# A token mixer behind gated linear attention on one core: u of batch 1 turned by DMA transposes, decays of batch 1 from products, and a new instruction list

## The chip, the cores and the metric

The kernel runs on one core of a Trainium2 chip. The metric is the device time of one execution in microseconds; smaller is better. The core has TensorE (PE, with its weight loads shown as PEld), VectorE (DVE), ScalarE (ACT), GpSimd (POOL) and SyncE (SP), each with its own instruction queue that runs in order, and 16 DMA engines that they share.

## The reference

Two stages follow each other. The first is a recurrent attention with a gate for each key channel; the second is an MLP-mixer block over its output.

```python
B, H, S, D = 4, 8, 768, 48
f = 1 / (1 + exp(-f_logit))
for t in range(S):
    state = f[:, :, t, :, None] * state + einsum('bhd,bhe->bhde', k[:, :, t], v[:, :, t])
    y[:, :, t] = einsum('bhd,bhde->bhe', q[:, :, t], state)
x = y.transpose(0, 2, 1, 3).reshape(B, S, H * D)              # (4, 768, 384)
h = maximum(x.transpose(0, 2, 1) @ w_tok1, 0) @ w_tok2        # 768 -> 256 -> 768
u = x + h.transpose(0, 2, 1)
out = u + maximum(u @ w_ch1, 0) @ w_ch2                       # 384 -> 1536 -> 384
```

Inputs and output are float32. Matmuls run in bf16 with float32 sums.

## The kernel before

**Attention.** The 768 steps are cut into six chunks of 128. Within a chunk the recurrence is closed: running sums of the log gates (a product with a triangle of ones, "sums") give G = exp(-sum) and Gi = exp(sum), q*G and k*Gi are formed ("gated"), both are turned by TensorE ("turn", then "turned" copies them from PSUM), their product ("scores") is masked by the triangle ("masked", AmT), and y is masked scores times v plus the turned q times the state before the chunk ("y", written as two bf16 blocks that "spread" makes, state_bd). The state goes on as `tsum = state + parts`, `state = tsum * glast`, where glast is the decay over the whole chunk. The log gate is kept as a bf16 high part and a low part ("lo", Llo, line 374), so "sums" has two matmuls of 384 columns (lines 456 and 457).

**Two ways to get the decay of a chunk.** If (batch, chunk) is in `TOTALS`, "sums" also has eight one-column matmuls against a column of ones (lines 450 to 455), and a small ScalarE exp of the result is glast (line 480). If not, ScalarE takes the exp of the last 32 rows of the sums ("grow", line 472) and a DMA from SP brings its last row into the form of glast (line 476). Before, only batch 0 is in `TOTALS`; it runs in pairs of chunks (`PAIRS`, function `pair`), with two-column matmuls of the same kind (line 607).

**Mixer.** For each batch: tok1 (line 750, 12 matmuls of 384 columns), h1T = relu (a copy from PSUM; batch 0 in two halves of 192 columns), tok2 (line 766), u = x + tok2 (line 782), u_bf in bf16, u turned to uT, ch1 (line 819, 24 groups of three matmuls), zT = relu (lines 352 and 354), ch2 (line 838, in pieces of four matmuls), the last sum (line 844) and a store from SP. For batches in `UTURN` u is turned by two DMA transposes from SP (line 795), each for three row blocks: the first for 0 to 2, the second for 3 to 5. For the others TensorE turns it by 18 transposes (line 804), which VectorE or ScalarE copy to uT.

**What sets the order.** Every step is recorded as an Op with the engines that can do it. The string `ORDER` lists them all once, by number, in one sequence. A letter behind a number picks the engine (A for ScalarE, D for VectorE, G for GpSimd), numbers behind colons the PSUM banks. `Plan.run` (line 123) issues the steps in that sequence, so each engine runs its own steps in the listed order; semaphores keep the dependences. So the list of one batch's mixer is interleaved with the attention of the next. The token `zN` stands for N filler matmuls of 512 columns (line 870) whose result nobody reads: 13 at the start and 17 more in the first 26 us.

**Loads.** q, k, v, f of batches 1 to 3 and the weights come by DMAs that GpSimd issues in list order; f of batch 0 comes from SP. Before anything else, constants are made (triangle, identity, masks, zeroed paddings), most of them by VectorE (lines 277 to 324).

Of the kernel before, what the change touches and what calls it, by code (L numbers as in the profile page):

```python
# [9 lines left out]
FP32 = mybir.dt.float32  # L10
# [5 lines left out]
NBANK = 8  # L16
RING = 16384
KEPT = 3
UTURN = (2, 3)
# [3 lines left out]
TOTALS = [(0, 0), (0, 1), (0, 2), (0, 3), (0, 4), (0, 5)]  # L23
# [4 lines left out]
POOLED = ()  # L28
LOADS0F = [('f', (0, 2)), ('f', (2, 4)), ('f', (4, 6))]
# [10 lines left out]
216:6 157 209 67 158 136A z3 193:2:5 164A 217 66 198 192:4:1 170 z1 161:0:2 63 196 195 197 z6 166 194:4 171A 172G 341  # L40
173 200 199:5:1 167A 201 174D 202A 203G 204 210 347 218 71 205D 206 338 211 219 207D 342 212 220 339 213 343G 221 214D
215A 222A 223D 232:3 344 168D 228:4 340G 233 348 229 240 234 224:0 345 241 68 230 244 225 243A 236 252:6 226 242A
250:7 349G 237 245 253D 251A 360:5 231 239A 248:6 346G 256:7 362 249D 368:4 238D 257A 272:6 65 246A 235 280:2 273A 227
254:3 363 396:7 281D 404:0 255A 364 247D 258:6 370 259A 262:2 74 361 270:1 263D 350 69 266:6 369 16 284:2 73 399 264:5
285D 400 260:3 72 271D 265A 302:2 267A 373 300:1 353 70 365 371 374:6 301D 354 48 366:5 372 375D 303A 306:1 261A 75
286:2 398 307D 296:3 367D 287A 355G 378:1 397 377:2 407 381 376:7 76 389 408 304:4 380 276:1 78 305A 388 274:7 405 387
383G 282:4 382A 351 79 278:2 379 283A 294:6 406 401 77 288:5 352D 295A 290:0 275A 409 402:6 277A 289D 291A 384:7 403D
292:1 386A 410:0 279A 390 293D 393:5 297A 392G 298:2 80 395A 411D 433:3 299A 394D 412:1 391G 436 413:4 385D 81 414:5
435 437 416 268:2 434 471:7 417 464:3 269A 424 441:1 472 328:2 425 313:0 415 418 323:4 426 420G 438 421:6 419G 324 82
427 423A 442 430:5 422A 84 325 432D 431A 465 443 439:6 83 326 473 444 314 440A 88 449:4 428A 445:1 452 86 429A 315  # L50
446D 466 453 447:4 448:5 454A 455G 451 467 85 329 450 474 318:4 87 459 456:6 460 319 457A 458D 461:5 316 468 475 462D
308:6 589 356 469 476 320 590 470D 586 477D 330 463D 587 493:7 598 321 481:5 588G 592 331 478:3 595 484:4 479 89 490:0
596 309 482 591D 483A 333:1 485 599 310 494 480A 486G 491 334 495G 597D 604:5 97 600D 487:3 605 496:0 500:7 606 94
498:4 497D 612:2 501D 492A 335 499D 614 488 593 510:4 609 615 530:3 594G 336 613 506:7 311 522:0 511A 93 601 617 610:2
523A 508:4 90 607 640:6 509D 608 518:0 641 91 611D 616 618:4 507A 516:1 531D 489A 92 519A 619D 648:5 504:3 517A 502:7
98 505D 643 620:0 503D 621:1 823 644 622:3 632 96 642 524:7 649 623 534:1 95 650 624 526:6 544:2 357 535D 527A 514:0
631 824 528:6 525A 515D 820 628:4 645 536:7 529A 630D 677:1 545A 646:6 625 537A 546:2 633 651 627G 647D 678 358 532:7
652 629A 653 540:0 626A 533D 547A 656:3 634 541A 658:4 680 654:2 661 659 602 636G 512:0 681 635A 99 520:7 679 662
637:5 513A 660 603G 554:1 655A 670 550:0 682 664G 556:6 639A 663G 521A 657:4 638A 693:3 668 555A 665:7 685:5 832 669
715:2 557 686 551D 687 683:4 667D 666A 708:5 688 829 538:0 671 821 558 539D 673A 822G 833 674:7 696 559 826 689:0 359  # L60
684A 716 548:3 690D 542:6 675D 676A 838:1 825D 543A 709 692:7 672A 549D 691:6 830 704 710 827 571:3 695 561:7 694 711
717 703 845:6 566:4 847 697 839 699G 700:0 846 831G 718 567 701D 841 848 562 698G 842 840 849 572 835 843 332 702D
705:1 327 552:6 706A 707D 317 712 719 828D 553A 844 576:0 720 713 573 721A 714D 872:2 574 722:5 875 737:6 850 731:3
876 738 734:1 851 563 723 739A 735 724A 577 732 736A 581:1 564 733G 834D 728:3 741 582 729 725:7 730A 568 726 874 583
727A 569 836 740 854:3 584 853:4:7 852:5:6 864 879:1 578 855 880 881 784:4 863 873 780:6 579 882 766:2 857 877 772:0
858G 865 907:1 878 773A 770:7 785A 774:0 767A 771D 760:4 859A 312 781D 910 786:7 322 761D 869:6 866 787A 762:4 856
868A 867G 775A 756:2 884 860:5 757A 744:0 885 908 778:7 745D 862A 886:2:3 837D 861A 911 888:0 763A 776:5 883 891 909
890 782:4 777A 892 750:1 779A 900 894G 768:5 783D 751A 893G 752:0 871A 889 914:4 753A 912 742:1 916 870D 895:0 769A
748:3 915 913 746:5 749A 887:4:6 897A 747D 921:7 337 758:2 898 575 788:5 899 759A 936:6 896A 810:3 789D 743A 917 943:0
904:5 919:1:4 918 905D 944 811 922 945 901 937 570 812 924 903A 902G 923 580 938 946 925 764:7 927G 754:1 765A 800:4  # L70
906A 755D 926A 920:5:7 939 932 795:1 931 928:2 801 929D 933:7 947 940 934A 935D 802 948 941 796 949A 942A 790:0 930A
959:6 965:5 950:2 966 962:7 797 967A 963 815:5 960 964G 951 961A 791 952A 969 816 956:6 953:7 957 805:2 565 798 958G
792 954 813 806 955G 803 817 968 793 807 1000:3 1004:7 1016:1 1005A 994:6 1001A 1017D 1002:7 818 1010:1 1003A 819
1014:5 1011D 794 986:7 1015D 799 976:1 987A 585 974:5 996:7 975D 982:3 808 980:5 995D 983A 809 1008:2 981D 560 998:6
977D 984:3 997D 999A 988:1 985A 972:6 989D 978:3 1009D 973A 970:1 1012:2 971A 990:6 1013D 1048:1 1006:7 991A 979A
1033:5 1007A 1038:3 1043:6 1034 1039 1023:7 1018:0 992:2 1049 1044 993A 1050 1040 1051 1052 1028:2 1041 1045 1042 1024
804 1035 814 1025 1036 1029 1046 1026 1047 1019 1027 1030 1037 1020 1031 1032 1021 1022
# [15 lines left out]
class Plan:  # L93
# [52 lines left out]
def kernel(  # L146
# [125 lines left out]

    def once(name, engine, fn, make, own, need=()):
# [16 lines left out]
    once("ident0", DVE, lambda: nc.vector.tensor_copy(ident[:, 0:1], tri_bf[:, 0:1]), ["ident"], 70, ["tri_bf"])  # L290
# [19 lines left out]
    if PAIRS:  # L310
# [3 lines left out]
        for n, rows in ((0, lo64), (1, hi64)):  # L314
            memset(f"half2{n}", half2[rows, n:n + 1], 1.0, ["half2"], 60)
            once(f"inc2{n}", DVE, lambda rows=rows: nc.vector.tensor_copy(inc2[rows, rows], tri_bf[rows, rows]), ["inc2"], 130,
                 ["tri_bf"])
            once(f"pmask0{n}", DVE, lambda rows=rows: nc.vector.tensor_copy(
                pmask[0][rows], tri_bf[rows, rows].unsqueeze(2).broadcast_to((64, 64, 2))), [("pmask", 0)], 200, ["tri_bf"])
        once("exc2", DVE, lambda: nc.vector.tensor_tensor(exc2, inc2, ident, ALU.subtract), ["exc2"], 150, ["inc2", "ident"])  # L320
        once("pmask1", DVE, lambda: nc.vector.tensor_copy(pmask[1], pmask[0]), [("pmask", 1)], 160, [("pmask", 0)])
        for n, rows in ((0, lo64), (1, hi64)):
            once(f"pmask1{n}", DVE, lambda rows=rows: nc.vector.tensor_copy(pmask[1][rows, :, 0], exc2[rows, rows]),
                 [("pmask", 1)], 130, ["exc2"])
# [16 lines left out]

    def copy_on(eng, out_, in_):
        if eng == ACT:
            nc.scalar.activation(out_, in_, AF.Copy, bias=0.0, scale=1.0)  # L344
        elif eng == DVE:
# [558 lines left out]
```

## Time and profile before

| what | us |
| --- | --- |
| median of 3 runs | 173.82 |
| lowest and highest | 173.77, 174.5 |
| span of the profiled execution | 172.8 |
| TensorE busy in the span | 164.4 |
| VectorE, ScalarE, GpSimd busy | 129.1, 109.7, 78.0 |

The profiled execution is shown by its span, from its first instruction to its last, 172.8 us; the median of the timed runs is 1.0 us above it, for what lies around the span. Sums in the prediction are made against the span and then moved by that 1.0. Columns of a group row: busy us in all, mean ns of one instruction, then the idle time of the engine just before them and what ended it. A row of a table of stretches gives for each stretch its length and, for each engine, busy us and number of instructions, then the granted clock, the DMA share and GB/s. Matmul durations include the drain of the pipeline, so the cost of a matmul in a row of them is read from start to start.

### The profile page before, as it was taken

The page shows a single profiled execution, that of the slowest core. Times are in us where ns is not written, and L with a number is a line of the kernel's source. Part 1 is how long each engine was busy: PE and PEld are TensorE (multiplying, and loading weights), DVE is VectorE, ACT ScalarE, POOL GpSimd, SP SyncE. Part 2 cuts the span into 40 slices and gives each one's busy share as a digit, 9 for nine tenths or more (in the row PEclk, how much of TensorE's full clock was granted, in tenths as well). Part 3 has the DMA queues.
Part 4 walks back from the last instruction along what each step waited for, and adds up shares of the span by engine and source line. Part 5 has one row for each costly group of instructions (what it writes and reads, how often), then busy time and mean ns, then how long its engine had stood idle before and what let it go on. Part 6 is the DMA issues. An engine that isn't in the chain of part 4 may idle for free.

```text
span 172.8 us, 4455 instructions
## 1 busy us (share of the span) xinstructions
PE 164.4 (95%) x1758; PEld 103.6 (60%) x1762; DVE 129.1 (75%) x287; ACT 109.7 (64%) x246; POOL 78.0 (45%) x102
## 2 busy tenths in 40 slices
PE   6889998999999999999999999999999999999991
PEld 2465755566676666676667566666565656656660
DVE  6989996978997789989969859887786355581132
ACT  3997938999893656799999685479933430444100
POOL 2999846998566893799663330010101012000000
PEclk9999999999999999999999999999999999999999
DMA  5999999999997998999999995638155006250054
GB/s 146 217 169 175 246 210 210 157 122 129 197 134 154 182 109 197 133 60 114 108 135 69 63 141 135 144 81 157 32 154 154 1 19 163 89 188 0 2 200 168
DMA packets 89573, 22.74 MB, mean 132 GB/s; under 512 B 82288, under 2 KB 88736, under 8 KB 89552
## 3 DMA queue, kind: packets, MB, share of 16 engines
q0 software_dynamic: 69600, 13.77, 91.7%
q1 hardware_dynamic: 19952, 8.69, 19.6%
q8 instruction: 14, 0.23, 0.6%
q14 instruction: 7, 0.06, 0.1%
HBM read 25.17 MB, written 4.72 MB: 173 GB/s over the span
## 4 chain that ended last, share of the span: by engine, by line
PE 75%; ACT 8%; DVE 5%; issue 1%; DVEq 0%
PE ps L838 26%; PE ps L819 23%; PE ps L750 4%; PE ps L766 4%; PE ps L408 3%; ACT zT L352 2%; PE ps L495 2%; PE ps L456 2%; PE ps L560 2%; PE ps L457 1%; ACT L L367 1%; PE ps L870 1%; PE ps L424 1%; PE ps L804 1%; PE ps L556 1%
## 5 line engine op out<-in xcount | busy, mean ns | idle before, releaser
L838 PE MATMUL ps<-w_ch,zT 128*128 128x384 bf16 (+2 forms) x300 | 52.9, 319 | 0.0
L819 PE MATMUL ps<-uT,w_ch 128*128 128x384 bf16 x288 | 52.4, 326 | 0.3 <-ACT GG L468 0.2
L352 ACT ACTIVATE zT<-ps 128x384 bf16<-128x384 f32 x61 | 28.2, 493 | 19.6 <-PE ps L819 14.6
L838 PEld LDWEIGHTS <-zT 128*128 128x128 bf16 x300 | 28.4, 98 | 17.4 <-issue 0.2
L819 PEld LDWEIGHTS <-w_ch 128*128 128x128 bf16 x288 | 26.9, 97 | 17.0 <-issue 0.7
L354 DVE TENSOR_SCALAR zT<-ps 128x384 bf16<-128x384 f32 x35 | 18.9, 554 | 10.4 <-PE ps L819 8.9
L536 DVE TENSOR_TENSOR AmT<-ps,tri_bf 128x512 bf16<-128x512 f32 x36 | 23.1, 683 | 2.3 <-PE ps L408 2.1
L348 POOL CAST state_bd<-state 48x192 bf16<-48x192 f32 x24 | 9.0, 376 | 34.6 <-DVE state L549 22.2
L844 DVE TENSOR_TENSOR x_nat<-x_nat,ps 128x384 f32<-128x384 f32 (+2 forms) x25 | 12.8, 534 | 10.3 <-PE ps L838 9.8
L264 POOL DMA_DIRECT2D qk_sb<-in_q_dram x16 | 15.9, 1000 | 0.8 <-issue 0.8
L264 POOL DMA_DIRECT2D qk_sb<-in_k_dram x16 | 15.7, 983 | 0.3 <-issue 0.3
L264 POOL DMA_DIRECT2D v_sb<-in_v_dram x16 | 15.7, 983 | 0.1
L782 DVE TENSOR_TENSOR x_nat<-x_nat,ps 128x384 f32<-128x384 f32 x21 | 10.8, 549 | 4.2 <-PE ps L766 4.1
L750 PE MATMUL ps<-x_bf,w_tok 128*128 128x384 bf16 x48 | 13.2, 326 | 0.3 <-DVE zT L698 0.2
L348 POOL CAST u_bf<-x_nat 128x384 bf16<-128x384 f32 x6 | 3.0, 506 | 20.7 <-DVE x_nat L782 20.7
L374 POOL TENSOR_TENSOR Llo<-L 128x384 bf16<-128x384 f32 x10 | 8.2, 826 | 6.4 <-ACT L L367 6.3
L485 DVE TENSOR_TENSOR qk<-qk_sb,GG 128x768 bf16<-128x768 bf16 x18 | 9.9, 555 | 1.4 <-ACT GG L468 1.4
L870 PE MATMUL ps<-x_nat 128*128 128x512 bf16 x26 | 8.7, 460 | 2.0 <-DVE x_nat L279 1.5
L466 ACT ACTIVATE GG<-ps 128x384 bf16<-128x384 f32 x18 | 8.7, 492 | 2.5 <-PE ps L457 2.3
L344 ACT ACTIVATE x_bf<-ps 128x384 bf16<-128x384 f32 x13 | 6.5, 499 | 5.9 <-PE ps L560 5.0
L766 PE MATMUL ps<-h1T,w_tok 128*128 128x384 bf16 x48 | 9.4, 326 | 0.8 <-ACT h1T L352 0.6
L468 ACT ACTIVATE GG<-ps 128x384 bf16<-128x384 f32 x18 | 8.9, 492 | 1.8 <-PE ps L457 1.6
(96 smaller groups left out, 266.4 us busy)
## 6 DMA issues: line engine op xcount, KB each, us to landing
out_dram<-x_nat SPq DMA_DIRECT2D x23, 192.0 KB, 2.2
f_sb<-in_f_logit_dram POOLq DMA_DIRECT2D x3, 1152.0 KB, 11.1
f_sb<-in_f_logit_dram SPq DMA_DIRECT2D x3, 384.0 KB, 4.2
w_ch<-in_moe_w_ch_dram POOLq DMA_DIRECT2D x2, 576.0 KB, 13.2
qk_sb<-in_q_dram POOLq DMA_DIRECT2D x12, 96.0 KB, 6.6
qk_sb<-in_k_dram POOLq DMA_DIRECT2D x12, 96.0 KB, 5.6
v_sb<-in_v_dram POOLq DMA_DIRECT2D x12, 96.0 KB, 4.5
w_ch<-in_moe_w_ch_dram POOLq DMA_DIRECT2D x1, 1152.0 KB, 10.0
```

What stands on the lines that cost most here:

```text
L264: lambda eng=eng, into=into, of=of: eng.dma_start(out=into, in_=of),
L348: nc.gpsimd.tensor_copy(out_, in_)
L352: nc.scalar.activation(out_, in_, AF.Relu, bias=0.0, scale=1.0)
L354: nc.vector.tensor_scalar(out_, in_, 0.0, None, ALU.max)
L536: add(("masked", b, c, p), DVE, lambda half=half, made=made: nc.vector.tensor_tensor(half, made(), tb4, ALU.mult), need=["tri_bf"], make=[ ...
L750: add(("tok1", b, rt, kt), PE, lambda rt=rt, kt=kt, pm=pm: nc.tensor.matmul(banks[pm.at][:, 0:DM], lhsT=w_tok1[:, kt, rt * 128:(rt + 1) * ...
L766: nc.tensor.matmul(banks[pm.at][:, 0:DM], lhsT=w_tok2[:, kt, tt * 128:(tt + 1) * 128], rhs=h1T[:, kt, :], start=(kt == 0 and not held), st ...
L782: nc.vector.tensor_tensor(to, un, banks[pm.at][:, 0:DM], ALU.add)
L819: nc.tensor.matmul(banks[pm.at][:, 0:384].rearrange("p (n t) -> p n t", t=128), lhsT=w[:, kt, c0:c0 + 128], rhs=uT[:, rows3, kt, :], start ...
L838: nc.tensor.matmul(banks[pm.at][:, 0:n1 - n0], lhsT=zT[:, kt, tt * 128:(tt + 1) * 128], rhs=w_ch2[:, kt, n0:n1], start=(kt == 0), stop=(kt ...
L844: add(("sum", b, tt, n0), DVE, lambda un=un, pm=pm, n=n1 - n0: nc.vector.tensor_tensor(un, un, banks[pm.at][:, 0:n], ALU.add), make=[("x_n ...
L870: nc.tensor.matmul(banks[NBANK - 1][0:rows, 0:cols], lhsT=steady[:, 0:rows], rhs=steady[:, 0:cols], start=True, stop=True)
```

## The change

- `UTURN` takes in batch 1: its u is turned by two DMA transposes from SP, and its 18 transposes and six copies to uT go.
- `TOTALS` takes in chunks 0 to 4 of batch 1: five times eight one-column matmuls and a small exp come, five grow steps and their five DMAs go. The paddings that these matmuls read are zeroed by new memsets.
- h1T of batch 0 is copied in whole rows (two copies of 384 columns in place of four of 192).
- The step state = tsum * decay may be listed for GpSimd; the list does so for chunks 2, 3 and 4 of batch 0 and chunk 1 of batch 2.
- Memsets may be listed for GpSimd, and copies among the constants for ScalarE.
- A token `wN` is one float32 filler matmul of N columns; it takes the place of the bf16 fillers at the start. The new list starts with `w512 w512 w384 s16` (`s16`: sixteen of 64 columns) and has no other filler.
- `ORDER` is another list throughout.

```diff
-UTURN = (2, 3)
+UTURN = (1, 2, 3)
-TOTALS = [(0, 0), (0, 1), (0, 2), (0, 3), (0, 4), (0, 5)]
+TOTALS = [(0, 0), (0, 1), (0, 2), (0, 3), (0, 4), (1, 0), (1, 1), (1, 2), (1, 3), (1, 4), (0, 5)]
+HALVES = False
+STATES = (DVE, POOL,)
...
     def memset(name, tl, value, make, own):
-        once(name, DVE, lambda: nc.vector.memset(tl, value), make, own)
+        op = once(name, (DVE, POOL), None, make, own)
+        op.fn = lambda: (nc.gpsimd if op.engine == POOL else nc.vector).memset(tl, value)
+
+    def copied(name, out_, in_, make, own, need):
+        op = once(name, (DVE, ACT), None, make, own, need)
+        op.fn = lambda: copy_on(op.engine, out_, in_)
...
+    def decayed(b, c, gb, key):
+        op = add(("state", b, c), STATES, None, need=["tsum", key], make=["state"], kind=("el", HP * D, True, 1))
+        op.fn = lambda: (nc.gpsimd if op.engine == POOL else nc.vector).tensor_tensor(state, tsum, gb, ALU.mult)
...
-            half = DM // 2 if b == 0 else DM
+            half = DM // 2 if b == 0 and HALVES else DM
...
     def idle(n, cols):
+        if not cols:
+            wide = spare[:, 0:512].bitcast(FP32)
+            nc.tensor.matmul(banks[NBANK - 1].rearrange("p (a n) -> p a n", n=128)[:, 0:n // 128], lhsT=wide[:, 0:128],
+                             rhs=wide[:, 0:128].unsqueeze(1).broadcast_to((128, n // 128, 128)), start=True, stop=True)
+            return
```

The two lists by stretch, each from the first tok2 of a batch to that of the next, as numbers of steps on an engine (before, then after):

| list up to | TensorE | VectorE | ScalarE |
| --- | --- | --- | --- |
| tok2 of batch 0 | 47, 50 | 74, 75 | 43, 55 |
| tok2 of batch 1 | 94, 86 | 63, 57 | 63, 58 |
| tok2 of batch 2 | 94, 91 | 69, 71 | 76, 75 |
| tok2 of batch 3 | 76, 78 | 50, 53 | 47, 35 |
| the end | 60, 60 | 30, 32 | 16, 12 |

Ahead of tok2 of batch 0 TensorE's new list has sums of chunks 0, 1 and 2 of batch 1 more. GpSimd's loads, in the order of the two lists:

```
before: q k v | k q q v v k of batch 0, w_tok1, f.1, w_tok2, w_ch1 (2), q.1.0 q.1.1 k.1.1 k.1.0 ...
after:  q k v | q k v k q of batch 0, f.1, k.1.0, v.0.4, w_tok1, w_tok2, q.1.0 k.1.1 q.1.1, w_ch1 (2), ...
```

SP's list around the new transposes: `glast.2.0 ut.1.0 glast.2.1 ut.1.1 glast.2.2 glast.2.3 store.0.0`.

More of the change, by code (lines that the diff above doesn't have):

```diff
@@ L40 @@
[L40 to L44, printed above, removed]
@@ L78 @@
+1015
 """
@@ L271, in load_w, with copy_on @@
             make=[name], kind=("load", 900, 1024, size))
+    def copy_on(eng, out_, in_):
+        if eng == ACT:
+            nc.scalar.activation(out_, in_, AF.Copy, bias=0.0, scale=1.0)
+        elif eng == DVE:
+            nc.vector.tensor_copy(out_, in_)
+        else:
+            nc.gpsimd.tensor_copy(out_, in_)
     def once(name, engine, fn, make, own, need=()):
@@ L548, in rest @@
                     need=["state"], make=["tsum"], bank=p_d, kind=small)
-                add(("state", b, c), DVE, lambda: nc.vector.tensor_tensor(state, tsum, gb, ALU.mult),
-                    need=["tsum", ("glast", g4)], make=["state"], kind=small)
+                decayed(b, c, gb, ("glast", g4))
             spread(b, c)
@@ L729, in pair @@
                         need=["state"], make=["tsum"], bank=p_d[k], kind=small)
-                    add(("state", 0, c), DVE, lambda gb=gb: nc.vector.tensor_tensor(state, tsum, gb, ALU.mult),
-                        need=["tsum", ("gpair", i2)], make=["state"], kind=small)
+                    decayed(0, c, gb, ("gpair", i2))
                 spread(0, c)
```

105 lines of the change are left out of this document (50 added, 55 removed).

## The prediction

> **What bounds the kernel now.** I read the busy totals first, then the chain that ended last, then a table cut where each batch's second token product (tok2, L766) begins: 30.0, 66.1, 104.9 and 137.8 us; the last matmul ends by 169.2.
>
> ```profile
> PE 164.4 (95%) x1758; PEld 103.6 (60%) x1762; DVE 129.1 (75%) x287; ACT 109.7 (64%) x246; POOL 78.0 (45%) x102
> PE 75%; ACT 8%; DVE 5%; issue 1%; DVEq 0%
> core 0: us, PE busy (x) PEld busy (x) DVE busy (x) ACT busy (x) POOL busy (x), PEclk, DMA share, GB/s
> 0.00:30.00 30.00, 25.80 (x451) 15.73 (x456) 25.02 (x74) 21.67 (x44) 21.92 (x33) 1.00 1.36 196
> 30.00:66.10 36.10, 35.77 (x382) 23.21 (x382) 31.36 (x64) 28.55 (x67) 29.43 (x36) 1.00 1.76 146
> 66.10:104.90 38.80, 38.52 (x402) 25.26 (x400) 32.84 (x70) 31.75 (x73) 22.35 (x26) 1.00 1.61 119
> 104.90:137.80 32.90, 32.90 (x325) 20.21 (x323) 25.11 (x51) 20.18 (x47) 2.76 (x7) 1.00 0.48 103
> 137.80:169.20 31.40, 31.39 (x205) 19.20 (x203) 14.26 (x29) 7.57 (x16) 1.53 (x3) 1.00 0.31 100
> ```
>
> From 30 us on TensorE is busy 99%: there time is TensorE work, and only less work saves any. Before 30 us it is busy 25.80 of 30.00, part of that with the fillers of L870; VectorE (25.02) and ScalarE (21.67) set that start. So I take two sums: T, when tok2 of batch 0 starts, and TensorE's work behind T.
>
> **Work behind T.** The costs, start to start:
>
> ```profile
> 71.16 0.50 PE ps L804 x9
> 145.76 10.72 PE ps L819 x66
> 9.52 0.17 PE L607 MATMUL ps<-x_nat,L 128*128 128x2 bf16 x1
> 9.89 0.16 PE L607 MATMUL ps<-x_nat,Llo 128*128 128x2 bf16 x1
> ```
>
> A transpose costs 0.50/9 = 0.056 us, a 384-column matmul 10.72/66 = 0.162, so a ch2 piece of four 0.65 and the two matmuls of a sums step 0.33. A two-column matmul costs (9.89-9.52)/15 = 0.025. Eighteen transposes of batch 1 go: -1.0. Five totals of eight one-column matmuls come: 40 x 0.025 = +1.0. The named edits cancel on TensorE; the list decides. Counting each list between its tok2 starts:
> - batch 0 to 1: three sums steps fewer (now ahead of T), -1.0; two totals, +0.4; five ch2 pieces fewer, -3.25: 36.1 becomes 32.25.
> - batch 1 to 2: two ch2 pieces more, +1.3; one sums step more, +0.33; transposes -1.0: 38.8 becomes 39.4.
> - batch 2 to 3: three ch2 pieces more, +1.95; one sums step fewer, -0.33: 32.9 becomes 34.5.
> - batch 3 to the end: the same 60 steps, 31.4.
>
> The sum falls from 139.2 to 137.6: **-1.6 us**. It comes from three sums steps with totals being done ahead of T, in holes.
>
> Is it still TensorE that sets these stretches? Prices of what changes engine:
>
> ```profile
> L354 DVE TENSOR_SCALAR zT<-ps 128x384 bf16<-128x384 f32 x35 | 18.9, 554 | 10.4 <-PE ps L819 8.9 <-ACT x_nat L344 1.5
> L346 DVE COPY qkT<-ps 128x1024 bf16<-128x1024 bf16 x9 | 6.2, 686 | 0.4 <-PE ps L495 0.4
> L485 DVE TENSOR_TENSOR qk<-qk_sb,GG 128x768 bf16<-128x768 bf16 x18 | 9.9, 555 | 1.4 <-ACT GG L468 1.4
> L346 DVE COPY uT<-ps 128x384 bf16<-128x384 bf16 x7 | 2.2, 352 | 0.3 <-PE ps L804 0.2
> L374 DVE TENSOR_TENSOR Llo<-L 128x384 bf16<-128x384 f32 x8 | 4.4, 561 | 0.0
> L374 POOL TENSOR_TENSOR Llo<-L 128x384 bf16<-128x384 f32 x10 | 8.2, 826 | 6.4 <-ACT L L367 6.3
> L468 ACT ACTIVATE GG<-ps 128x384 bf16<-128x384 f32 x18 | 8.9, 492 | 1.8 <-PE ps L457 1.6
> L472 ACT ACTIVATE grow<-ps 32x384 f32<-32x384 f32 x15 | 7.1, 482 | 1.0 <-PE ps L457 0.7
> L625 ACT ACTIVATE gpair<-ps 128x8 f32<-128x8 f32 x3 | 0.6, 205 | 0.0
> ```
>
> Other 384-column copies and sums on VectorE I take at 0.55 too. From batch 0 to 1 it has eight steps fewer (three x_nat, two of the 1024-column turns, one each of u, product, sum, h1T and memset go; a zT, an x_bf and two uT come), 3.8 us: 27.5 of 32.25 us, 85% (87% now). From batch 1 to 2 four zT, a sum, a turn, an x_bf, a product and a memset come, five uT, a Llo and a state product go, +2.3: 35.1 of 39.4, 89% (85% now). ScalarE sheds five grow steps (-2.4) for five small ones (+1.0) and nine zT. So TensorE still binds, with VectorE close behind in the second stretch.
>
> **The u transfers of batch 1.**
>
> ```profile
> L795 SPq DMA_TRANSPOSE uT<-u_bf x4: 1283/1289/1294, 108.6 to 144.3; - x4
> DMA to landing us min/median/max: 2.8/2.8/2.9
> ```
>
> In the new list SP has glast.2.0, ut.1.0, glast.2.1, ut.1.1. From tok2 of batch 1 at 0, at half a microsecond a step: ScalarE's ln.2.0 ends at 0.9, VectorE's lo.2.0 and three u at 2.9, GpSimd's two u_bf at 3.9, ScalarE's four gate steps, grow.2.0 and u_bf.1.0 at 3.4; SP issues at about 4, and it lands 2.8 later, at 6.8. Before the first ch1 of batch 1 the list gives TensorE twelve tok2 matmuls (1.9), ten ch2 pieces (6.5), five sums steps (1.7), three turns of eight (1.3) and scores, parts and a y (some 1.5): 13 us. The second transfer waits for u_bf.1.3 on ScalarE (8.4) and for u_bf.1.5 behind a 2.2 us issue on GpSimd; it lands near 11.3, its first reader is near 18. So it is hidden; without that cover the first would cost up to 6.8. Behind ut.1.1 on SP stand glast.2.2 and stores, not due soon.
>
> **T.** What binds the start:
>
> ```profile
> 4.26 0.84 ACT L387 ACTIVATE f_sb<-f_sb 128x768 f32<-128x768 f32 x1 [2.24 <-DMA f_sb<-in_f_logit_dram]
> 26.13 0.36 ACT L344 ACTIVATE state_bd<-state 48x192 bf16<-48x192 f32 x1 [3.07 <-PE ps L736]
> 9.88 1.17 DVE L629 TENSOR_TENSOR qk<-qk_sb,GG 128x384 bf16<-128x384 bf16 x4 [0.64 <-DMA qk_sb<-in_k_dram]
> 9.88:30.00 20.12, 17.79 (x42) 1.00 1.46 205
> L730 DVE TENSOR_TENSOR state<-tsum,gpair 128x192 f32<-128x192 f32 x4 | 1.4, 354 | 0.2
> L367 ACT ACTIVATE L<-f_sb 128x384 f32<-128x384 f32 x18 | 9.0, 517 | 0.2
> ```
>
> ScalarE's list ahead of T grows from 43 steps to 55: four more G and Gi (2.0), four constants (taken at 0.25, between the 0.205 and 0.492 of the rows above; 1.0), three exp and ln (1.55), a glast, a spread, the full-row h1T less an x_bf (0.45), 5.0 in all: 26.7 busy. Three of the constants lie in the 2.24 us before the first exp, leaving 0.74 at the start and 1.5 there idle: 28.9 if it never waits again. It waited 5.3 us in 6-30 (24.0-18.7), 3.07 of them at 26.13, where nothing else was ready; the new list puts f of batch 1 earlier, so that exp can go there. With the other 2.2 left, 31.1. VectorE: three state products (-1.1), two half h1T (-0.7) and twelve constants (-2.6 by their durations) go, five Llo (2.7), an x_bf, an x_nat and a product of batch 1 (1.65) and ten short memsets (1.1) come: 26.1 busy; 2.65 idle before 9.88 (9.88 less 25.02-17.79), and none to 2.33 of its later idle: 28.8 to 31.1. Both engines give the same ends; I take the middle, less a little because k of batch 0 is issued about 0.5 us earlier: **T = 29.8**, -0.2.
>
> State products on GpSimd: by the Llo pair 0.354 x 826/561 = 0.52 us each, between 0.35 and 0.83; three, off the longest lists. The Trainium skill's page GPSIMD Engine Reference (§3.1 Elementwise) puts a two-input tensor_tensor there at 1.96 times VectorE, against 1.47 by the rows; the estimate by the page would be 0.69 each and, were the last of them exposed, 0.2 us more.
>
> The full-row h1T has sums.1.2 (0.5) beside it, against a 0.65 us TensorE wait now:
>
> ```profile
> 29.99 2.07 PE L766 MATMUL ps<-h1T,w_tok 128*128 128x384 bf16 x10 [0.65 <-ACT h1T L352]
> ```
>
> I cost the hand-overs I can't see at what the old list loses by such waits: nothing net. Constants on three engines end before the first exp: nothing, below and above 0.4.
>
> **Sum.** 172.8 - 0.2 - 1.6 = 171.0 us of span. The median of the three runs is 173.82, 1.0 above the span: **172.0 us**. A measurement of this kernel can tell about 0.5% from no change, 0.87 us.
>
> **Rivals.** (1) *Loads take the place of the waits removed.*
>
> ```profile
> 13.18 0.83 POOL L270 DMA_DIRECT2D w_tok<-in_moe_w_tok_dram  x1
> w_tok<-in_moe_w_tok_dram POOLq DMA_DIRECT2D x1, 384.0 KB, 6.8
> 13.99 2.23 POOL L264 DMA_DIRECT2D f_sb<-in_f_logit_dram  x1
> f_sb<-in_f_logit_dram POOLq DMA_DIRECT2D x1, 1152.0 KB, 11.3
> ```
>
> w_tok1 landed at 20.0, f of batch 1 behind it at 25.3, 5.3 us later. Now f and one k go first: w_tok1 lands at 20.0 + 5.3 + 0.5 = 25.8, less the earlier start. tok1 is due near 25 with sums.1.0 and the last y behind it on TensorE; past about 26.5 each us late is one of T. Speaks for it: the queue is never empty there (DMA share 1.36 in the first row); against: 0.7 us of room. At T = 31.3: 173.5.
> (2) *Slower: VectorE becomes the bound from batch 1 on.* If it idles 18% instead of the 11% that the count leaves (it idled 15% there), 35.1/0.82 = 42.8 against 39.4, and 27.5/0.82 = 33.5 against 32.25: +4.7, **176.7**. It decides from 11% idle in the second of these stretches; with the 15% of now the time is 173.9, and past 16% in both the kernel is slower than before by more than 0.5%. For it: 89% full, in strict list order, and TensorE waits for each zT and mask. Against: VectorE's idle time now has sources that go with TensorE's own pace (8.9 us of zT waits on L819), so a shorter list there need not idle as much.
> (3) *Slower: the matmul clock.* The later fillers go, the first are float32.
>
> ```profile
> 1.46 4.72 PE L870 MATMUL ps<-x_nat 128*128 128x512 bf16 x13 [1.46 <-DVE x_nat L279]
> L870 PE MATMUL ps<-x_nat x26: 378/379/634, 1.5 to 25.5; 128*128 128x512 bf16 x26
> 6.00:30.00 24.00, 4.13 (x14) 1.41 (x17) 1.00 1.52 197
> ```
>
> The first fillers took 634 ns and later ones 378: TensorE starts slow. At one pass the float32 ones last about 0.6 us, at four about as long as the thirteen; I take four. Of the 25.80 us busy ahead of T the fillers are 4.13 after 6 us and some 4.5 before, which leaves 17 us of real matmuls; half pace all through makes them 34 in a stretch of 24, 10 more: 182. A single spell of 3.5 us, as long as the slow start, costs at most 1.75, within what the forecast gains; it decides from the third on. The Trainium skill's TensorE: Matmul & The Clock Gate (Part 1) says half rate returns after an idle window of about 3.4 us; by that rule, no hole here is long enough, and the row's longest wait now, 0.65 us, agrees.
> (4) *The holes close more fully*: T = 28.9 and the waits of the old list gone (0.9): 170.2.
>
> **How the numbers follow.** Forecast 172.0: 0.50 (its own range 171 to 173.5); loads 0.20; VectorE 0.16; clock 0.04; fuller 0.10. Faster by over 0.5%: most of the forecast and of (4), a little of (1): 0.62. Within: 0.19. Slower: 0.19, most of (2) and all of (3). The range goes from T at its lower end, 170.0, into the VectorE case, 175.4; left out are a tenth above and less below.
>
> **What would show it.** tok2 of batch 0 near 29.8, with three sums steps of L456 and L457 before it; no L804 past 40 us; stretches of 32.3, 39.4, 34.5, 31.4; no wait of L819 on a transfer at batch 1; w_tok1 landing before 26.5. Wrong if VectorE's share passes 90% from batch 1 to 2 while TensorE drops below 98%, or if matmuls of 384 columns start 0.32 us apart for long.

## The result and the profile after

| | us |
| --- | --- |
| after, median of 4 runs (lowest, highest) | 184.78 (184.34, 185.72) |
| before, median of 4 runs | 174.16 |
| ratio of after to before, 95% interval | 1.0596 [1.0548, 1.0645] |
| span of the profiled execution after | 183.3 |

The changed kernel is 6.0% slower; the forecast was 172.0. Here and below, times are medians of all executions of a kernel, while ratios and intervals leave out the few that ran markedly slower than the kernel's others, such as one of 279.72 us at a granted clock of 0.56 in experiment 4. The same table of stretches as in the prediction, now of after, cut where tok2 of each batch begins (31.3, 72.9, 113.7, 148.05):

```profile
core 0: us, PE busy (x) PEld busy (x) DVE busy (x) ACT busy (x) POOL busy (x), PEclk, DMA share, GB/s
0.00:31.30 31.30, 26.37 (x476) 17.51 (x477) 25.60 (x76) 26.15 (x56) 26.34 (x44) 0.89 1.50 192
31.30:72.90 41.60, 33.63 (x374) 22.44 (x372) 27.97 (x58) 23.63 (x59) 29.19 (x32) 0.88 1.88 166
72.90:113.70 40.80, 39.20 (x394) 25.02 (x392) 35.12 (x71) 33.11 (x76) 19.76 (x25) 1.00 1.27 91
113.70:148.05 34.35, 33.92 (x335) 21.16 (x334) 25.96 (x53) 15.46 (x36) 3.11 (x8) 1.00 0.46 102
148.05:179.50 31.45, 31.39 (x205) 19.20 (x203) 15.50 (x31) 5.59 (x12) 2.43 (x5) 1.00 0.26 83
```

The prediction had 29.8, 32.25, 39.4, 34.5, 31.4. The last two are right, the first and third took 1.5 and 1.4 longer, and the second took 9.35 longer: TensorE is busy 33.63 of 41.60 there and the granted clock falls to 0.88. TensorE's two largest waits of after (columns: engine and what it makes, what it waited for, us in total, times, longest):

```profile
PE ps L560 <- POOL state_bd L281: 8.0, 1, 8.0
PE ps L462 <- POOL Llo L379: 1.6, 1, 1.6
```

GpSimd's own waits in after that stand before a load ("issue": what ended the wait is not named by the view):

```profile
POOL qk_sb L266 <- issue: 5.9, 2, 3.6
POOL qk_sb L266 <- DMA f_sb<-in_f_logit_dram: 4.4, 1, 4.4
POOL qk_sb L266 <- DMA w_ch<-in_moe_w_ch_dram: 3.7, 3, 1.9
...
POOL w_ch L272 <- DMA f_sb<-in_f_logit_dram: 1.5, 1, 1.5
```

One y (L560, chunk 3 of batch 1) waits 8.0 us for a GpSimd copy of the state (L281), and GpSimd, which waited for no transfer at all in the kernel before, waits for f of batches 1 and 2 and for weights. A load is named by tensor, batch and chunk: q.2.1 is q of batch 2, chunk 1; f.2.0 and q.3.0 bring a whole batch at once. spread.1.2.48 is the copy in question, of the state behind chunk 2 of batch 1. The chain that ended last (start, us, what) shows why:

```profile
43.84 14.17 DMA f_sb<-in_f_logit_dram
58.01 0.28 issue
58.29 0.87 POOL qk_sb L266
...
59.76 0.84 POOL v_sb L266
...
60.65 0.34 POOL state_bd L281
```

f.2.0 is issued at 43.84 and lands at 58.01; 0.28 us later GpSimd issues q.2.1. Nothing in q.2.1 needs f.2.0: in the built program GpSimd's loads use eight semaphores in turn, and the issue of a load first waits for the one of the load eight places ahead. (In all sixteen traces no load goes out before the landing of the eighth ahead, and one held for it goes out 0.28 to 0.46 us behind it.) From f.2.0 the list goes v.2.0, k.2.1, v.2.1, k.2.2, q.2.0, k.2.0, q.2.2, q.2.1: the eighth. The copy spread.1.2.48 stands behind it in the list and runs at 60.65, though its input was ready at 51.8:

```profile
51.46 0.36 DVE L577 TENSOR_TENSOR state<-tsum,glast 128x192 f32<-128x192 f32 x1
```

Of these 8.8 us GpSimd was held 5.3 before the issue of k.2.0, q.2.1 and v.2.2; the other 3.5 are the time that four issues took, 0.87 us each. The clock row of after (40 slices of 4.6 us):

```profile
PEclk9999958999996579999999999999999999999999
```

It shows half pace twice: at 22 to 28.8, and from 56.2 to 66.3, behind the 8 us hole, where TensorE's work from 61.04 on still runs at 0.50.

### The profile page after: what moved, and what is told of

It reads as the page before. It is cut to its first block, busy times and chain, and to the rows that moved or that the text cites. A ratio compares the mean times of both kernels' runs of the same rounds, so it can differ in the third digit from the quotient of the medians.

```text
span 183.3 us, 4478 instructions
## 1 busy us (share of the span) xinstructions
PE 164.5 (90%) x1776; PEld 105.3 (57%) x1776; DVE 130.7 (71%) x289; ACT 103.9 (57%) x236; POOL 80.8 (44%) x112
## 3 DMA queue, kind: packets, MB, share of 16 engines
HBM read 25.17 MB, written 4.72 MB: 163 GB/s over the span
## 4 chain that ended last, share of the span: by engine, by line
PE 48%; DMA 24%; POOL 18%; issue 6%; DVE 1%; POOLq 0%; DVEq 0%
PE ps L845 20%; PE ps L826 16%; DMA f_sb<-in_f_logit_dram 15%; POOL qk_sb L266 10%; DMA w_ch<-in_moe_w_ch_dram 7%; POOL v_sb L266 5%; DMA qkT<-qk 3%; PE ps L757 2%; PE ps L773 2%; PE ps L413 2%; POOL u_bf L281 1%; PE ps L564 1%; PE ps L500 1%; PE ps L462 1%; PE ps L560 1%
## 5 line engine op out<-in xcount | busy, mean ns | idle before, releaser
L845 PE MATMUL ps<-w_ch,zT 128*128 128x384 bf16 (+2 forms) x300 | 52.8, 320 | 0.0
L357 ACT ACTIVATE zT<-ps 128x384 bf16<-128x384 f32 x52 | 24.5, 495 | 21.9 <-PE ps L826 21.5
L359 DVE TENSOR_SCALAR zT<-ps 128x384 bf16<-128x384 f32 x44 | 23.2, 552 | 8.1 <-PE ps L826 7.4
L281 POOL CAST state_bd<-state 48x192 bf16<-48x192 f32 x18 | 6.4, 354 | 28.5 <-DVE state L577 17.2
L281 POOL CAST u_bf<-x_nat 128x384 bf16<-128x384 f32 x12 | 6.3, 553 | 14.1 <-issue 12.1
L379 POOL TENSOR_TENSOR Llo<-L 128x384 bf16<-128x384 f32 x9 | 7.4, 827 | 11.7 <-ACT L L372 11.6
L277 ACT ACTIVATE state_bd<-state 48x192 bf16<-48x192 f32 x22 | 7.9, 360 | 7.8 <-DVE state L577 7.1
L560 PE MATMUL ps<-state_bd,qkT 128*128 128x96 bf16 x60 | 5.1, 210 | 8.0 <-POOL state_bd L281 8.0
L277 ACT ACTIVATE x_bf<-ps 128x384 bf16<-128x384 f32 x10 | 4.8, 483 | 12.7 <-PE ps L564 12.7
L471 ACT ACTIVATE GG<-ps 128x384 bf16<-128x384 f32 x18 | 8.9, 497 | 3.4 <-PE ps L462 3.4
L577 DVE TENSOR_TENSOR state<-tsum,glast 128x192 f32<-128x192 f32 x11 | 3.9, 354 | 8.6 <-POOL state_bd L281 7.7
```

What stands on the lines that cost most here:

```text
L281: nc.gpsimd.tensor_copy(out_, in_)
L357: nc.scalar.activation(out_, in_, AF.Relu, bias=0.0, scale=1.0)
L359: nc.vector.tensor_scalar(out_, in_, 0.0, None, ALU.max)
L845: nc.tensor.matmul(banks[pm.at][:, 0:n1 - n0], lhsT=zT[:, kt, tt * 128:(tt + 1) * 128], rhs=w_ch2[:, kt, n0:n1], start=(kt == 0), stop=(kt ...
```

## Experiments

The tokens are written by their names; only GpSimd's list is shown where only that changes. spread is a copy of the state and lo the low half of the log gate, as above; behind a time stands the ratio to the kernel before, run beside it, or its 95% interval in brackets. "Queue theory": the order of GpSimd's list is the cause. Rivals: the clock (fillers gone, float32 start), the extra transfers of u, and the supply of the DMA engines whatever the order.

**1. Loads behind the copies.**

```diff
-spread.1.1.0 q.2.0 k.2.0 q.2.2 q.2.1 v.2.2 spread.1.2.48 f.3.0 v.2.5 spread.1.3.0
+spread.1.1.0 spread.1.2.48 spread.1.3.0 q.2.0 k.2.0 q.2.2 q.2.1 v.2.2 f.3.0 v.2.5
```

> The changed kernel, with seven of GpSimd's loads (q.2.0, k.2.0, q.2.2, q.2.1, v.2.2, f.3.0, v.2.5) put behind its copies spread.1.1.0, spread.1.2.48 and spread.1.3.0, which they stood ahead of. Nothing else is moved, and no work is left out. Queue theory: GpSimd stood still because a load could not be issued before the eighth load ahead of it had landed (q.2.1 was issued at 58.29, f.2.0 had landed at 58.01), so the copy spread.1.2.48 ran at 60.65 and TensorE stood for 8.0 us; with the copies ahead TensorE's gap at 52.8 falls under 1 us, the half-clock stretch behind it (56.2 to 66.3) goes, and the time falls by 8 to 10.5 us, to 174.5 to 177. Clock theory (the removed fillers and the float32 start cost the time): the gap closes for 8 us, but GpSimd's delay comes back at the loads that are now later, and under 4 us are won. Transfer theory (the extra transfers of u fill the DMA queues and make all loads late): the loads land as late as before, batch 2 waits for them, under 3 us are won.

Measured: 186.52, ratio 1.0673 [1.0619, 1.0727]. The hole at 52.8 was gone, and the time was not better. TensorE's longest wait, and then the chain from 68 us on:

```profile
PE ps L462 <- POOL Llo L379: 12.8, 1, 12.8
```

```profile
68.59 3.85 issue
72.44 1.73 POOL qk_sb L266
...
79.12 2.37 issue
81.49 2.22 POOL qk_sb L266
...
84.67 0.80 POOL Llo L379
...
85.50 0.48 PE ps L462
```

The hole moved to GpSimd's next result that TensorE needs, lo.2.3 (L379), which now stood behind k.3.0 (72.44) and q.3.0 (81.49), each held before its issue. The expectation of the queue theory was wrong in its number: one hole was repaired, and the list had the same fault again 20 us later. Nothing was won, as the two rivals allowed (under 4 and under 3 us), so this run excluded neither.

**2. Fillers back, alone and with the first edit.**

```diff
+z4 scores.0.2 ... z3 scores.0.4 ... z1 scores.0.5 ... z2 within.0.2
```

> The changed kernel with ten filling matmuls of 512 columns put back on TensorE: four ahead of scores.0.2, three ahead of scores.0.4, one ahead of scores.0.5, two ahead of within.0.2, which is where TensorE stood for 1.05, 0.65, 0.30 and 0.78 us between 19.7 and 23.9. No work is left out. Both theories expect the granted clock to stay at 1.00 from 22 to 28.8 us, where it was 0.50, and the first matmul of tok2 to start 1.5 to 2.5 us earlier than 31.33. Queue theory: the gap at 52.8 ends with the landing of f.2.0 (58.01) and not with TensorE's own work, so it grows by what was won, and the time stays within 0.7 us of 184.8. Clock theory: the time falls by 1.5 us or more.

> The two edits before together (the seven loads behind the copies, the ten filling matmuls): no work is left out. Queue theory: now what the fillers win is kept, 1 to 2.5 us beyond the first of the two alone: 172.5 to 175.5. Clock theory: the sum of what each gives alone. If the fillers win nothing here either, the half clock from 22 to 28.8 us was not on the path.

Measured: 185.55 [1.0616, 1.067] alone, 187.42 [1.0701, 1.0783] with both, where the hole of experiment 1 is there again (12.7 us). Of the run with fillers alone, the clock row, the row of tok2 (shortest, median and longest ns, first and last start) and TensorE's longest wait:

```profile
PEclk9999999999997569999999999999999999999999
```

```profile
L773 PE MATMUL ps<-h1T,w_tok x48: 325/326/326, 31.0 to 152.9; 128*128 128x384 bf16 x48
```

```profile
PE ps L560 <- POOL state_bd L281: 9.0, 1, 9.0
```

The clock stayed full through 28.8 us, the first tok2 came at 31.0 in place of 31.3 (1.5 to 2.5 had been expected), and the hole grew from 8.0 to 9.0. The time rose by 0.8 where the queue theory allowed 0.7 and the clock theory asked for 1.5 less. So the half clock at 22 us is worth 0.3 us of the start here, and what is won ahead of the hole is lost in it.

**3. The same trap in the kernel before.** Nine loads of batch 2 go ahead of one copy:

```diff
-f.2.0 spread.1.2.48
+f.2.0 v.2.0 k.2.1 v.2.1 k.2.2 q.2.0 k.2.0 q.2.2 q.2.1 v.2.2 spread.1.2.48
```

> The kernel before, with nine of its loads of batch 2 (v.2.0, k.2.1, v.2.1, k.2.2, q.2.0, k.2.0, q.2.2, q.2.1, v.2.2) put ahead of GpSimd's copy spread.1.2.48; nothing of the change is in it, and no work is left out. Queue theory: the eighth of them waits for the landing of f.2.0 (about 61.6), so the copy runs at 63 to 64 in place of 54.06 and TensorE stands for 5 to 9 us near 56, with a half clock behind it: 180 to 187. Rivals: the loads are issued without a wait of GpSimd, the copy comes 8 us of issue time later at most, and the time stays under 177.

Measured: 183.93, ratio 1.0553 [1.0509, 1.0598]. Its wait, and GpSimd at the held load and the copy behind it:

```profile
PE ps L556 <- POOL state_bd L348: 7.5, 1, 7.5
```

```profile
59.72 0.88 POOL L264 DMA_DIRECT2D qk_sb<-in_q_dram  x1 [1.64 <-DMA f_sb<-in_f_logit_dram]
...
61.55 0.74 POOL L348 CAST state_bd<-state 48x192 bf16<-48x192 f32 x2
```

With nothing else of the change, this order alone costs 9.4 us. The load held is again the eighth behind f.2.0. The copy came at 61.55 (54.06 before), a little earlier than expected. But of the some 8.4 us for which it stood behind its input (ready at 53.1) only 1.64 are the held issue; the rest is the time to issue the loads ahead of it, 0.87 us each. So this run shows what the order costs, and mostly by the issue time, as the rival had it for the copy; what the rival gave for the time, under 177, was wrong.

**4. Batch 3 behind too, without and with fillers.**

```diff
-f.3.0 v.2.5 v.2.3 q.2.4 k.2.3 q.2.3 k.3.0 k.2.5 v.2.4 q.2.5 k.2.4 u_bf.1.1 u_bf.1.2 q.3.0 u_bf.1.5 u_bf.1.4 lo.2.3 v.3.0 lo.2.4 spread.2.0.0
+v.2.5 v.2.3 q.2.4 k.2.3 q.2.3 k.2.5 v.2.4 q.2.5 k.2.4 u_bf.1.1 u_bf.1.2 u_bf.1.5 u_bf.1.4 lo.2.3 lo.2.4 f.3.0 k.3.0 q.3.0 v.3.0 spread.2.0.0
```

> The changed kernel with the seven loads behind the three copies as in the first experiment, and besides the four loads of batch 3 (f.3.0, k.3.0, q.3.0, v.3.0) behind GpSimd's low halves lo.2.3 and lo.2.4, which they stood ahead of. No work is left out. Queue theory, corrected: the hole was not closed in the first experiment but moved to GpSimd's next result that TensorE needs (lo.2.3, 12.8 us late at 72.35, since k.3.0 waited for the landing of f.3.0 and q.3.0 for k.3.0); with batch 3 behind, GpSimd has that result near 71 to 74, the hole falls from 13 to under 3 us, the half-clock stretch behind it goes, and the time comes to 172 to 176. Supply theory (the DMA engines, full until about 83 us, are the limit, whatever the order): the hole opens again at another place, and the time stays above 180.

> The run before this one with the ten filling matmuls of the second experiment as well (four ahead of scores.0.2, three ahead of scores.0.4, one ahead of scores.0.5, two ahead of within.0.2). No work is left out. The first tok2 started at 31.33 without and at 30.8 to 31.0 with the fillers, though the clock was full: the clock from 22 to 28.8 us costs 0.3 to 0.5 us of the start and no more, so with the later holes gone the time falls by 0.3 to 0.5 us against the run before it. Clock theory: by 1.5 us or more.

Measured: 188.86 [1.0731, 1.09] and 188.5 [1.076, 1.0866]. The hole moved once more; without fillers, TensorE's wait and the chain:

```profile
PE ps L560 <- POOL state_bd L281: 14.0, 1, 14.0
```

```profile
75.92 2.21 POOL qk_sb L266
78.13 7.44 issue
85.57 2.21 POOL qk_sb L266
...
91.15 0.36 POOL state_bd L281
```

The number of the queue theory was missed, and the supply theory's, above 180 with a hole at another place, was met; but the run showed a second limit. The DMA issues of this stretch give f.3.0, issued at 73.65, 11.6 us to its landing, so 85.2:

```profile
f_sb<-in_f_logit_dram POOLq DMA_DIRECT2D x1, 1152.0 KB, 11.6
```

q.3.0 was issued right behind that, though f.3.0 stands only two places ahead. What they have in common is size: a whole batch is 128 rows x 8 heads x 6 chunks = 6144 packets, and q.3.0 would have been the third such load under way. In after, too, k.3.0 (71.48) and q.3.0 (80.94) were held by a load six and five places ahead. So GpSimd's issue seems to be held by two things: the landing of the eighth load ahead, and too many packets under way. The held q.3.0 would have brought the loads not yet landed to 18432 packets here (three times 6144) and to 16384 in after (2 x 6144 and 4 x 1024, the loads of one chunk); in the 173.12 kernel of experiment 6 it went out at once, with 14336 (2 x 6144 and 2 x 1024). A limit between 14336 and 16384 fits every load of the sixteen traces, but no run varied it; it stays argued.

**5. By due time.**

```diff
 (the order of experiment 1, and)
-k.3.0 k.2.5 ...        +q.2.5 k.2.4 behind lo.2.4
-q.3.0 u_bf.1.5 ...     +k.3.0 behind spread.2.1.48, q.3.0 behind spread.2.2.0
-lo.2.3 v.3.0 lo.2.4    +v.3.0 behind lo.3.4
 (second kernel, besides)  +w_ch1.1 w_ch1.0 v.1.1 v.1.0 behind spread.0.4.48
 (third kernel, besides)   +the ten fillers
```

> The changed kernel with GpSimd's loads of batches 2 and 3 put where nothing that TensorE needs soon stands behind a load that must wait: the seven loads behind spread.1.3.0; q.2.5 and k.2.4 behind lo.2.4; k.3.0 behind spread.2.1.48; q.3.0 behind spread.2.2.0; v.3.0 behind lo.3.4. No work is left out. In the last run but one the hole moved to 79.4 (14.0 us, on spread.2.0.0), where q.3.0 had waited 7.4 us: the load eight places ahead of it had landed at 69.7, but it was issued at 85.57, right behind the landing of f.3.0 at 85.21, the one that would make three loads of 6144 packets under way. Queue theory: with at most two of them under way and both limits kept from what is due, all three holes go (8.0, 12.8 and 14.0 us), the clock stays full behind 30 us, and the time comes to 172 to 175. Supply theory: another hole of over 5 us opens and the time stays above 180.

> The run before this one, and besides w_ch1.1, w_ch1.0, v.1.1 and v.1.0 behind spread.0.4.48, so that GpSimd's products state.0.3 and state.0.4 and its copies of batch 0 no longer stand behind loads that wait for the landing of f.1.0 (22.6). No work is left out. Queue theory: the first tok2 starts at 29 to 30 in place of 31.3 and the time falls by 1 to 2 us against the run before it. Load theory (the landing of w_tok1 at 25.9 and TensorE's work behind it bound the start): it starts within 0.4 us of 31.3.

> The run before this one with the ten filling matmuls ahead of scores.0.2 (four), scores.0.4 (three), scores.0.5 (one) and within.0.2 (two). No work is left out. Queue theory: with GpSimd out of the way, TensorE's own pace from 22 to 28.8 us (granted clock 0.50 without fillers) is what is left of the start, and the fillers now win 0.5 to 2 us, more than the 0.3 to 0.5 us of the start that they won behind GpSimd's waits. Load theory: nothing.

Measured: 181.58 [1.0384, 1.0489]; 182.39 [1.045, 1.0591]; 183.82 [1.0544, 1.0618]. All three missed the queue theory's times. In the first, the three holes were gone and TensorE's longest wait had another owner, and v.3.0 has this row among the DMA issues:

```profile
PE ps L429 <- DMA v_sb<-in_v_dram: 4.4, 1, 4.4
PE ps L826 <- DMA uT<-u_bf: 1.6, 1, 1.6
```

```profile
v_sb<-in_v_dram POOLq DMA_DIRECT2D x1, 576.0 KB, 14.0
```

v.3.0 was now issued too late (96.86, 14.0 to landing). The edits of the start moved it nearly as was said, but won no time: first tok2 at 30.9, 30.3 (29 to 30 had been expected) and 29.8 in the three, with the later loads pushed back.

**6. v.3.0 earlier.**

```diff
-lo.2.4 q.2.5 k.2.4 spread.2.0.0 spread.2.0.48 state.2.1 lo.2.5 spread.2.1.48 k.3.0 lo.3.3 lo.3.0 lo.3.1 spread.2.2.48 spread.2.2.0 q.3.0 lo.3.5 lo.3.4 v.3.0
+lo.2.4 k.2.5 v.2.4 spread.2.0.0 spread.2.0.48 q.2.5 k.2.4 state.2.1 lo.2.5 spread.2.1.48 k.3.0 q.3.0 lo.3.3 lo.3.0 lo.3.1 spread.2.2.48 spread.2.2.0 v.3.0 lo.3.5 lo.3.4
```

> The kernel ordered by due time (two calls ago), with GpSimd's q.3.0 right behind k.3.0 (behind spread.2.1.48), v.3.0 behind spread.2.2.0 in place of lo.3.4, k.2.5 and v.2.4 behind lo.2.4, q.2.5 and k.2.4 behind spread.2.0.48 (in the 3.5 us in which GpSimd waited for glast there). No work is left out. In that run v.3.0 was issued at 96.86 and landed at 110.84, and TensorE stood for 4.4 us at 106.5 waiting for it, with a clock below 1.00 for two slices behind it. Queue theory: the load now starts at 89 to 92 and lands before 104, the hole and the half clock go, and the time falls by 5 to 7 us to 174.5 to 176.5; what is then left against the kernel before is the wait for the turned u (1.6 us at 78). Supply theory: the DMA engines bring it no earlier than 109, and under 2 us are won.

> The run before this one with w_ch1.1, w_ch1.0, v.1.1 and v.1.0 behind spread.0.4.48 and the ten fillers of the second experiment. No work is left out. With both, the first tok2 had started at 29.79 (31.33 in the changed kernel), but the loads behind came later and lo.2.3 was waited for (1.9 us). Queue theory: lo.2.3 now stands ahead of two more loads, so that wait falls under 0.7 us, the earlier start is kept, and the time is 0.5 to 1.5 us under the run before it: 173 to 175.5. Otherwise the earlier start is lost again at the next load and the two agree within 0.5 us.

Measured: 173.12, ratio 0.9928 [0.9891, 0.9965]; with the edits of the start 175.67 [1.0023, 1.0109]. The first of these is the changed kernel with 14 of GpSimd's loads at other places and nothing else. It is 11.7 us faster than that kernel, more than was expected, and 0.7% faster than the kernel before, with an interval clear of 1. Its stretches from the first tok2 (31.12) on, its longest wait behind 30 us, and the landings of the turned u:

```profile
31.12:62.20 31.08, 31.08 (x373) 21.32 (x372) 27.52 (x58) 23.63 (x59) 22.72 (x26) 1.00 1.94 164
62.20:102.61 40.41, 39.45 (x394) 24.97 (x392) 35.72 (x71) 33.20 (x76) 26.66 (x31) 1.00 1.77 137
102.61:136.34 33.73, 33.73 (x334) 21.14 (x333) 26.03 (x53) 15.37 (x36) 3.13 (x8) 1.00 0.48 104
136.34:167.85 31.51, 31.40 (x206) 19.20 (x203) 15.52 (x32) 5.60 (x12) 2.44 (x5) 1.00 0.26 82
```

```profile
PE ps L826 <- DMA uT<-u_bf: 0.7, 1, 0.7
```

```profile
DMA to landing us min/median/max: 2.8/2.9/7.9
```

The second stretch falls from 41.60 to 31.08 at a full clock with the same steps on TensorE. So the supply of the DMA engines is not what limits that stretch: they are as full as in after (share 1.94, 1.88), and TensorE doesn't stand. With the start's edits the first tok2 came at 29.8, but the gain was not kept (tok1 of that kernel, then two of TensorE's waits):

```profile
L757 PE MATMUL ps<-x_bf,w_tok x48: 322/326/337, 26.2 to 137.2; 128*128 128x384 bf16 x48
```

```profile
PE ps L460 <- POOL Llo L379: 1.5, 1, 1.5
PE ps L826 <- DMA uT<-u_bf: 1.1, 1, 1.1
```

**7. The rest of the prediction's steps.** The first kernel is the last one above with q.1.5, v.1.3 and v.1.2 behind lo.1.4; the other two are the 173.12 kernel with one edit each:

```diff
-UTURN = (1, 2, 3)      +UTURN = (2, 3)
-ut.1.0 ut.1.1 (SP)     +ut.1.0 to ut.1.5 on TensorE, uT.1.0 to uT.1.5 on VectorE (4) and ScalarE (2)

-w512 w512 w384 s16     +z13
```

> The run with v.3.0 earlier and both edits of the start (the four loads behind spread.0.4.48, the ten fillers), and besides q.1.5, v.1.3 and v.1.2 behind GpSimd's low half lo.1.4. No work is left out. The run without the last edit began its first tok2 at 29.77 (31.12 without the edits of the start), but TensorE then stood for 1.5 us at 41.05 for lo.1.4, and the gain was lost. Queue theory: the hole at 41 goes, the start stays at 29.8, and the time is 171.5 to 173, 0 to 1.5 us under the 173.1 of the order with the start left as it was. Supply theory: another hole of over 1 us opens behind and the time stays at 174 or above.

> The run with v.3.0 earlier (173.12, ratio 0.993 to before), with u of batch 1 turned by TensorE as in the kernel before: eighteen transposes and six copies out of PSUM (three on VectorE, two there again or on ScalarE as banks come free) in place of the two transfers. No work is left out. The prediction held that the transfers take 1.0 us from TensorE and are hidden. In the run with v.3.0 earlier TensorE waits 0.72 us for ut.1.0 (issued at 68.81, landed at 76.33). If the transfers gain what was predicted less that wait, this run is 0.3 us slower; if the DMA engines' load by the transfers costs more, it is over 1 us faster; if VectorE and ScalarE were the scarce ones there, over 1 us slower.

> The run with v.3.0 earlier, with thirteen bf16 matmuls of 512 columns at the start, as in the kernel before, in place of the three float32 and sixteen narrow ones. No work is left out. The prediction took 0.2 us for the float32 start, and the granted clock was 1.00 up to 22 us with it. If so, this run agrees within 0.5 us; if the float32 products are what lets the clock fall at 22 us, the clock stays at 1.00 and the first tok2 is over 1 us earlier.

Measured: 175.88 [1.0016, 1.0091]; 177.2 [1.0085, 1.0186]; 174.17 [0.9928, 0.9985]. The first missed: the earlier start is not kept by this edit either, and which load would have to move for it stays open. With u by TensorE the time is 2.1% more than with the transfers, some 3.6 us (1.0136 against 0.9928), more than the 0.3 expected: the transfers are worth having here. In the traced execution 1.1 us of the difference lies ahead of the first tok2 (32.2 against 31.1), where the two lists agree. Its third stretch against the 40.41 above has 1.2 us more TensorE work, about the 1.0 of the transposes; the fourth takes 1.4 us longer:

```profile
63.31:105.38 42.07, 40.62 (x411) 26.21 (x410) 36.66 (x75) 33.89 (x78) 25.07 (x30) 1.00 1.47 104
105.38:140.55 35.17, 33.98 (x335) 21.06 (x334) 26.01 (x53) 15.33 (x36) 3.11 (x8) 1.00 0.46 112
```

How much of the rest belongs to the places chosen for the new steps was not tried. The bf16 start agrees with the float32 one within the intervals, and its clock falls at the same place, so the float32 products are not the reason:

```profile
PEclk9999956999999999999999999999999999999998
```

## Why the prediction was wrong

- **The step that failed** is "I cost the hand-overs I can't see at what the old list loses by such waits: nothing net". The new list put loads of batches 2 and 3 ahead of GpSimd's copies and low halves, and the issue of a load can itself wait. That cost 8.0 us at 52.8, 2.65 behind it (5.3 us, 61.0 to 66.3, at half clock) and 1.6 for lo.2.3 (L462 on L379): 12.3 as an estimate, against the 11.7 by which 173.12 lies under 184.78. That the order of GpSimd's list is the cause is shown from both sides: alone it makes the old kernel 9.4 us slower (experiment 3) and the new one 11.7 faster (experiment 6). How the loss divides between held issues and the time of the issues themselves is read from the traces: 5.3 and 3.5 of the 8.8 us in after, 1.64 and the rest of 8.4 in experiment 3. GpSimd's list should have been walked as SP's was, issue by issue.
- **The work behind T** (-1.6 us) had the right mechanism and nearly the right size. Once GpSimd is out of the way the four stretches are 31.08, 40.41, 33.73 and 31.51, in sum 136.7 against 137.6 predicted and 139.2 before; VectorE is busy 27.52 and 35.72 in the first two (27.5 and 35.1 were counted; the "eight steps fewer" of the first are six, ten less four). The stretches are off by -1.2, +1.0, -0.8 and +0.1, so that their sum came so near is in part luck. This kernel's 173.12 is 1.1 over the forecast: T is 1.3 later, the stretches are 0.9 shorter, and its profiled execution took 1.7 more than its span (173.32, 171.6) where 1.0 was taken. That 1.0 was the span of one execution against the median of three: wherever both are on record for one execution, the time is 1.7 to 2.0 above the span, so the span of 172.8 would belong to the slowest of the three, 174.5.
- **T** was forecast at 29.8 and came at 31.3. It can be had: with the loads behind spread.0.4.48 and the fillers it is 29.8 in all three runs. With the loads alone it is 30.3 (one run), with the fillers alone 30.6 to 31.0 (three), and 30.9 to 32.4 in the six kernels with after's list ahead of T; the two latest of these, 32.2 and 32.4, are those whose 6.8 us at half pace began at 23.9 and 24.3 in place of 22. So the two edits together are clear of that spread, and the share of each is not. The counts of ScalarE and VectorE were right (26.15 and 25.60 busy, 26.7 and 26.1 counted); what they left out is GpSimd, whose product state.0.3 stood behind w_ch1.1, held 1.5 us for the landing of f.1.0, and the half pace. The state products themselves take what was said (mean 511 ns; 0.52).

- **Rival 1** (loads) had T right, 31.3, by another mechanism: w_tok1 landed at 25.96 (issued at 14.13, 11.8 to landing), inside its bound of 26.5, and tok1 began at 26.2 in the run whose tok2 began at 29.8.

```profile
w_tok<-in_moe_w_tok_dram POOLq DMA_DIRECT2D x1, 384.0 KB, 11.8
```

- **Rival 2** (VectorE) did not happen: its share from batch 1 to 2 is 88% (35.72 of 40.41) with TensorE at 98%.
- **Rival 3** (the clock) was right that the clock falls without the later fillers. Its price, at most 1.75 us for 3.5, was far from reached: without the 6.8 us at half pace T came 0.3 us earlier in experiment 2. The float32 fillers lasted about as long as the thirteen, as taken (4.34 us against 4.72). The dear spell, 56.2 to 66.3, is a consequence of the hole. The prediction's "no hole here is long enough" did not hold; the last section has the rows.
- **The u transfers** are hidden in after, as said; with the holes gone they are not quite: "it lands 2.8 later" held for idle DMA engines (median 2.9), but behind GpSimd's loads ut.1.0 took 7.5 us (68.81 to 76.33), and TensorE waited 0.7.
- Small steps (totals, full-row h1T, constants) can't be told apart by these runs beyond the stretches' agreement.

## What to carry to other kernels

A DMA issue is an instruction that takes its own time (here 0.87 us for the load of one chunk) and that can wait, for reasons that have nothing to do with its own data; so whatever stands behind it in an in-order list inherits the landing of an older transfer. Walk such a list with its landings, and place each load between two bounds: far enough back that no result due soon stands behind a held issue, early enough that it lands in time (q.2.1 missed the first bound in after, v.3.0 the second in experiment 5). When a repair moves a hole and not the time, look for the same fault at the next hand-over before giving up the theory.

## What was not expected of the hardware

- The clock can fall without a long idle time. Cut on the 3.4 us grid on which the clock changes in after (22.0, 28.8, 56.2, 66.3), the stretch ahead of the first fall had TensorE busy 1.87 of 3.40, and its longest wait there was 0.9 us (L676 on zT); with the fillers it was 3.17, and the clock stayed. The table of stretches for after, and below it for the run with fillers alone and for the first run of experiment 4:

```profile
18.60:22.00 3.40, 1.87 (x60) 1.58 (x61) 2.98 (x8) 3.35 (x7) 1.50 (x3) 1.00 1.59 182
22.00:25.40 3.40, 2.67 (x77) 2.00 (x67) 3.40 (x7) 3.11 (x9) 2.47 (x4) 0.50 1.43 199
25.40:28.80 3.40, 3.40 (x70) 2.44 (x67) 2.73 (x7) 2.75 (x8) 3.14 (x7) 0.50 2.07 170
83.44:86.85 3.41, 1.89 (x17) 1.23 (x16) 1.47 (x3) 1.65 (x5) 3.41 (x4) 1.00 1.85 100
```

```profile
18.60:22.00 3.40, 3.17 (x56) 1.88 (x61) 2.98 (x8) 3.35 (x7) 1.52 (x3) 1.00 1.60 183
```

```profile
24.30:31.12 6.82, 6.82 (x96) 4.62 (x93) 4.94 (x13) 4.92 (x13) 6.50 (x12) 0.50 1.65 190
```

  A stretch busy 2.67 of 3.40 did not bring the clock back; behind a full one it was 1.00. Neither is a rule. A stretch of after that was as little busy, 1.89 of 3.41 at 83.4, kept the full clock behind it, and in experiment 4 two full stretches in a row, from 24.3 on, ran at half pace before it came back. What decides stays open. The Trainium skill's TensorE: Matmul & The Clock Gate (Part 1) has a free-running window of about 3.4 us and lets the clock fall after an idle one. The window length agrees; that the window must be idle does not, since the clock fell behind one that was 55% busy.
- GpSimd's issue was held up to 7.4 us. The Trainium skill's DMA: Bandwidth & Descriptors (Issuing engines are not separate DMA queues) says that the choice of the issuing engine saves only the time on its sequencer to start the transfer, usually small beside the transfer. For the issue itself the trace agrees: 0.87 us for q.2.1, and 5.8 from there to its landing. But GpSimd stood 4.4 us before that issue, and the copy behind it cost TensorE 8.0.
